# Batch 0's keys and values in eight transfers, the norm factor spread through the two row halves of TensorE, zero matmuls in the first waits, and a new order of all tasks

## The chip, the cores and the metric

The kernel runs on one core of a Trainium2 chip. The metric is the device time of one launch in microseconds. A core has TensorE (matrix products, "PE"; its weight loads are listed apart as "PEld"), VectorE ("DVE"), ScalarE ("ACT") and GpSimd ("POOL"). SyncE ("SP") computes nothing here and issues every DMA transfer.

## The reference

The reference chains two blocks over 8 batches of 576 positions. The first is a linear attention with 8 heads of width 64, followed by a norm over the width:

```
kv  = einsum('bhsd,bhse->bhde', k, v)
out = einsum('bhsd,bhde->bhse', q, kv)
out = out / sqrt(mean(out*out, axis=-1) + 1e-6) * g_norm
```

Its result, laid out as x (576 x 512 per batch), goes into the second block, a mixture of 4 attention experts of which each position uses 2:

```
logits = x @ w_gate                        # the top 2 of 4, softmax of the two
for e in range(4):
    q, k, v = x @ wq[e], x @ wk[e], x @ wv[e]        # 512 -> 64
    a  = softmax(causal(q @ k.T / 8))
    ye = a @ v @ wo[e]                               # 64 -> 512
    out += weight_of_e * ye
```

All inputs and the output are float32.

## The kernel before

Each batch is cut into some 120 named tasks, and the tasks of all batches are written out in three tables: `ORDER` is one sequence of all tasks, `ENGINE` says for each task which engine runs it, and `SLOTS` gives buffers and PSUM banks to the objects in the order in which they are begun. No scheduler moves anything afterwards. Every engine works through its own tasks in the sequence of the table and stands still at a task whose input is not there; SP does the same with its transfers. Most buffers exist twice (`POOLS`), so a transfer into a buffer waits until the last reader of the buffer's former content is done.

The tasks of one batch, with the line under which the profile shows them:

- `lk`, `lv` (line 373) and `lq` (380) load k, v and q. K and v lie with 64 row groups doubled over 128 partitions, so a load has two pieces of 1024 and 1280 bytes per row. Batches 1 to 7 load all 8 heads with each piece. Batch 0 has two parts (`k_parts`), and each part takes heads 0 and 1 (or 2 and 3) and heads 4 and 5 (or 6 and 7) in pieces of 2 heads: 16 transfers.
- `kv` (393) is the product k'v per head. Heads 0 to 3 go to the lower 64 columns of TensorE, heads 4 to 7 to the upper 64; consecutive matmuls alternate between the two. The profile counts two matmuls for each one in the program here. `kvc` and four `ks` (314 on ScalarE, 318 on VectorE) copy the result out of PSUM.
- `qt` (413) transposes half of q on VectorE, `out` (425) multiplies it with kv, `oc` (314, 318) copies the result to `oT`, and `sq` (447, 449) squares it.
- `gl` and `ms` (456) sum gate products and squares over the width. `ln`, `rs`, `na`, `nb`, `nc`, `yh`, `r2` (467 to 494) turn the sums into 1/rms, one Newton step included. The result `r` is 128 x 160: 8 heads x 4 strips on the partitions' rows, positions in strips of 32.
- `sp` (550), the spread, brings 1/rms onto the 128 rows of two heads: for each pair of heads four matmuls against a selection matrix `ssel`, one for each strip, of 128 rows and 160 columns. `xm` (563) multiplies it with `oT` on VectorE and gives `xT`.
- `qp`, `kp` (593) and `v` (575) are the projections, `sc` (616) the scores, with two experts in the two 64-row halves of TensorE, `exp` (628) and `msk` (636) the masked exponential, `pv` (649) its product with v, `rc`, `iv`, `os` (663 to 673) the scaling, `ot` (691) a transpose, `y` (707) the last product, `yc` its copy and `st` (715, 718) the store.

Before the first `kv` stand 12 matmuls on a tile of zeros (734), as `ZEROS` says. The weights are loaded by `lw` (346) and scaled by the norm's weights by `ws` (352, 354), six of them; `lwg`, `lg` and `wgs` do this for the gate.

Of the kernel before, what the change touches and what calls it, by code (L numbers as in the profile page):

```python
# [43 lines left out]
ENGINE = (
    "SSVSASVSVSVSASASVSPSSSSSSTTAVVAAVVTTAAVVAPVPTTAAVVVVVVVVVPAVVVVVTVTVTVTVTATATATATVTAPTAPTAPTAPTVVVTV"
    "VVTVTATATAPTAPTAPTAPTVPVTVVVTATASTASTVSTVSSSSSTAVAAAVVTTVPVPVAAATTAAAVVVVVVVVPAVVVVVTVTVTVTVTATVTATA"
    "TATAPTAPTAPTAPTVPVTVPVTATATVTAPTAPTAPTAPTVVVTVVVTVTASTASTVSTASTASSSSSTAVAVVVVTTVPAPAAAATTAAVVVAVVVVV"
    "PAVVVVVTVTVTVTVTATVTVTATVTAPTAPTAPTAPTVVVTVPVTATVTATAPTAPTAPTAPTVVVTVPVTATASTASTVSTASSSSSTVVVAVVVTTV"
    "AAPVAVATTAAVVVVVVVVVPAVVVVPTVTVTVTVTVTATVTVTVTAPTAPTAPTAPTVVVTVPVTVTATVTAPTAPTAPTAPTVPVTVVVTATASTAST"
    "ASTASTASSSSSTAAAVAVVTTAAAVVAAVTTAAAVVAVVVVVVAVPVVPTVTVTVTVTATVTATATVTAPTAPTAPTAPTVPVTVPVTATATATAPTAP"  # L50
    "TAPTAPTVPVTVVVTVTASTVSTASTASSSSSTAVVAVVVTTAVVPAPVATTAAVVVVVVVVVPAVVVVVTVTVTVTVTVTVTVTATATAPTAPTAPTAP"
    "TVPVTVVVTATATATAPTAPTAPTAPTVVVTVVVTATASTVSTASTVSTVSSSSSTAVAAVVVTTAAAAAPVVTTAAVVVAVVVVVVAVPVVVTVTVTVT"
    "VTVTVTATATATAPTAPTAPTAPTVPVTVVVTVTVTATAPTAPTAPTAPTVPVTVPVTATASTVSTASTASSSSSTVVVAAVVTTVVAPVVAATTAAVVV"
    "AVVVVVPAVPVVPTVTVTVTVTVTATATATATAPTAPTAPTAPTVVVTVVVTVTVTATATAPTAPTAPTAPTVPVTVVVTATATASTASTVSTASTAS"
)
# [10 lines left out]
def k_parts(b):  # L66
    return [(0,), (1,)] if b == 0 else [(0, 1)]
# [6 lines left out]
def names(nb):  # L74
# [5 lines left out]
    for b in range(nb):  # L80
# [6 lines left out]
        out += [(m, b) for m in ("r2", "glr", "glt", "lgs")]  # L87
# [12 lines left out]
def objects(n):  # L100
# [27 lines left out]
        "r2": lambda: [("sm", b), ("r2", b)],  # L128
# [35 lines left out]
def kernel(  # L164
# [614 lines left out]
```

## Time and profile before

| | us |
|---|---|
| median of 3 runs (223.63 to 227.99) | 224.07 |
| the profiled execution | 224.8 |
| its span, first to last instruction | 222.6 |
| TensorE busy / weight loads | 197.2 / 163.0 |
| VectorE, ScalarE, GpSimd busy | 144.4, 124.9, 54.1 |

The mean granted clock of TensorE is 0.951 of full speed. DMA moves 40.32 MB, 181 GB/s over the span. A busy time sums an engine's own work; matmuls overlap in their pipeline, so the share of a busy TensorE is not that of its peak. The chain of waits follows the end of the program back, at each step to what released it.

### The profile page before, as it was taken

Reading aid. Unit: us, or ns where it says so; the run is one execution under the profiler, and the core shown is the slowest. Engines: PE = TensorE matmul, PEld = TensorE weight load, DVE = VectorE, ACT = ScalarE, POOL = GpSimd, SP = SyncE. Lnnn points to the kernel's source line nnn. Section 1 sums busy time; section 2 is a strip of 40 time slices with the busy share of each in tenths; the row PEclk is TensorE's granted clock in tenths of the full one; section 3 lists DMA queues with packets and bytes.
Section 4 is the critical chain, followed back from the end, with each engine's and each line's share of the span. In section 5 each row is a group of like instructions: output and inputs, shape, how many; then the busy total and the mean of one; then the engine's idle time right before and its main releaser. Section 6 shows DMA issues by size and latency. Waiting matters only on the chain.

```text
span 222.6 us, 7257 instructions
## 1 busy us (share of the span) xinstructions
PE 197.2 (89%) x3030; PEld 163.0 (73%) x3044; DVE 144.4 (65%) x368; ACT 124.9 (56%) x222; POOL 54.1 (24%) x146
## 2 busy tenths in 40 slices
PE   7447749998999999999996999998999999999990
PEld 2235449686888878996895878987798869997850
DVE  5103974939769697947766887785685966663370
ACT  2001311676666773378634575377945887768951
POOL 3800400322512440004100253022410341333400
PEclk9855976999999999999999999999999999999998
DMA  6889989999942949597837714001014016004175
GB/s 189 234 222 271 377 178 325 356 334 377 334 170 76 343 141 314 190 299 232 291 62 257 257 50 140 19 3 52 1 70 168 3 40 198 3 0 144 68 271 183
DMA packets 31984, 40.32 MB, mean 181 GB/s; under 512 B 8656, under 2 KB 25040, under 8 KB 31952
## 3 DMA queue, kind: packets, MB, share of 16 engines
q1 hardware_dynamic: 31952, 39.86, 55.8%
q8 instruction: 24, 0.39, 0.8%
q14 instruction: 8, 0.07, 0.1%
HBM read 30.42 MB, written 9.44 MB: 179 GB/s over the span
## 4 chain that ended last, share of the span: by engine, by line
PE 65%; DMA 8%; DVE 7%; ACT 5%; issue 2%; SPq 1%; ACTq 0%; DVEq 0%
PE banks L593 14%; PE banks L616 7%; PE banks L550 7%; DMA v_b<-in_v_dram 7%; PE banks L575 7%; PE banks L456 6%; PE banks L649 6%; PE banks L425 6%; PE banks L393 6%; PE banks L707 5%; ACT PT L628 3%; DMA out_dram<-y 2%; PE banks L691 1%; DVE wgs L338 1%; DVE sq L449 1%
## 5 line engine op out<-in xcount | busy, mean ns | idle before, releaser
L628 ACT ACTIVATE PT<-banks 128x1024 bf16<-128x1024 f32 (+1 forms) x64 | 50.7, 837 | 10.8 <-PE banks L616 9.8
L636 POOL TENSOR_SCALAR_AFFINE_SELECT PT<-PT 128x256 bf16<-128x256 bf16 (+1 forms) x80 | 29.4, 391 | 56.6 <-ACT PT L628 52.9
L563 DVE TENSOR_TENSOR xT<-oT,banks 128x640 fp32r<-128x640 f32 x32 | 25.6, 815 | 12.3 <-PE banks L550 11.6
L393 PE MATMUL banks<-v_b,k_b 128*64 128x64 f32 x640 | 24.5, 241 | 6.3 <-DMA k_b<-in_k_dram 3.2
L393 PEld LDWEIGHTS banks<-v_b,k_b 128*64 128x64 f32 x640 | 22.9, 155 | 9.0 <-issue 7.3
L550 PE MATMUL banks<-r,ssel 128*128 128x160 f32 x128 | 21.3, 302 | 3.0 <-DVE r L494 3.0
L575 PE MATMUL banks<-wv_r,xT 128*128 128x256 f32 x160 | 22.9, 286 | 0.1
L413 DVE STREAM_TRANSPOSE qT<-q_b 128x1152 f32<-128x1152 f32 x16 | 21.8, 1365 | 1.6 <-DMA q_b<-in_q_dram 1.6
L425 PE MATMUL banks<-qT,kvx 32*64 32x288 f32 x256 | 20.5, 439 | 2.7 <-ACT kvx L314 1.6
L550 PEld LDWEIGHTS banks<-r,ssel 128*128 128x128 f32 x128 | 18.3, 208 | 6.1 <-DVE r L494 3.3
L616 PE MATMUL banks<-qs,kT 64*128 64x64 f32 (+4 forms) x192 | 21.4, 339 | 0.7 <-DVE kT L318 0.7
L593 PE MATMUL banks<-xT,wk_r 128*128 128x288 f32 x128 | 21.2, 306 | 1.0 <-DVE oT L318 0.5
L449 POOL TENSOR_TENSOR sq<-oT 128x576 f32<-128x576 f32 x11 | 12.6, 1152 | 34.5 <-DVE oT L318 18.7
L575 PEld LDWEIGHTS banks<-wv_r,xT 128*128 128x128 f32 x160 | 20.1, 189 | 0.9 <-ACT PT L628 0.7
L593 PE MATMUL banks<-xT,wq_r 128*128 128x288 f32 x128 | 20.5, 301 | 0.0
L593 PEld LDWEIGHTS banks<-xT,wk_r 128*128 128x128 f32 x128 | 17.8, 188 | 3.0 <-DVE oT L318 1.0
L425 PE MATMUL banks<-qT,kvs 32*64 32x288 f32 x256 | 19.8, 440 | 0.0
L616 PEld LDWEIGHTS banks<-qs,kT 64*128 64x128 f32 x192 | 14.3, 185 | 7.0 <-issue 0.9
L707 PE MATMUL banks<-wo_b,OT 128*128 128x512 bf16 x58 | 16.8, 380 | 2.8 <-ACT OT L314 1.9
L318 DVE COPY kvs<-banks 32x128 f32<-32x128 f32 x17 | 4.8, 285 | 21.9 <-ACT kvs L314 19.2
L314 ACT COPY kvs<-banks 32x128 f32<-32x128 f32 x15 | 3.9, 257 | 26.4 <-PE banks L393 19.6
L649 PE MATMUL banks<-vx,PT 128*128 128x65 bf16 x480 | 18.3, 193 | 0.2 <-DVE osc L673 0.2
(93 smaller groups left out, 310.2 us busy)
## 6 DMA issues: line engine op xcount, KB each, us to landing
q_b<-in_q_dram SPq DMA_DIRECT2D x16, 576.0 KB, 5.9
out_dram<-y SPq DMA_DIRECT2D x32, 256.0 KB, 2.4
v_b<-in_v_dram SPq DMA_DIRECT2D x7, 640.0 KB, 8.0
k_b<-in_k_dram SPq DMA_DIRECT2D x7, 640.0 KB, 7.8
v_b<-in_v_dram SPq DMA_DIRECT2D x7, 512.0 KB, 6.8
k_b<-in_k_dram SPq DMA_DIRECT2D x7, 512.0 KB, 6.8
out_dram<-y SPq DMA_DIRECT2D x8, 128.0 KB, 2.4
k_b<-in_k_dram SPq DMA_DIRECT2D x4, 160.0 KB, 4.1
```

The source lines that it names most:

```text
L393: nc.tensor.matmul(p_kv[c * Dh : (c + 1) * Dh, (2 * odd + r) * Dh : (2 * odd + r + 1) * Dh], lhsT=kv_in["k"][slot("k", b)][:, h, col], rhs ...
L413: nc.vector.transpose(qTs[slot("qT", b, h)][:].rearrange("p j d -> p (j d)"), q_in[slot("q", b, h)][:].rearrange("p j d -> p (j d)"),)
L425: nc.tensor.matmul(two("out", b, h, a // 2)[r * Dh : (r + 1) * Dh, a % 2, 0:n].rearrange("p (j g) -> p j g", g=NG), lhsT=kvx[rows, 2 * (a ...
L550: nc.tensor.matmul(p_s[:, s, 0:SW], lhsT=ssel[:, s, 2 * c : 2 * c + 2, :].rearrange("p h d -> p (h d)"), rhs=r2s[slot("r2", b)][:], start= ...
L563: nc.vector.tensor_tensor(out=by_strip(xTs[slot("xT", b)][:, c, :]), in0=by_strip(oTs[slot("oT", b)][:, c, :]), in1=p_s.rearrange("p s (i ...
L575: nc.tensor.matmul(bank("v", b, u)[:, n * E * Hd : (n + 1) * E * Hd], lhsT=x[:, c, i * P : (i + 1) * P], rhs=w_r["v"][:, c, :, :].rearrang ...
L593: nc.tensor.matmul(p_p[:, s, 0:HALF], lhsT=w_r[nm][:, c, 2 * pr : 2 * pr + 2, :].rearrange("p e f -> p (e f)"), rhs=x[:, c, s * HALF : (s ...
L616: nc.tensor.matmul(p_s[:, el, o : o + hi - lo], lhsT=kTs[slot("kT", b, pr)][pp, kb * P : (kb + 1) * P], rhs=qss[slot("qs", b, pr)][pp, lo:hi],
L628: nc.scalar.activation(PTs[slot("PT", b, pr)][:, :, d0 : d0 + o], two("sc", b, pr, j)[:, :, 0:o], ACTF.Exp, scale=scale)
L636: nc.gpsimd.affine_select(out=d, in_=d, compare_op=AluOpType.is_ge, fill=0.0, base=0, pattern=[[0, 2], [1, w]], channel_multiplier=-1,)
L649: nc.tensor.matmul(p_O[:, (2 * n + el) * (Hd + 1) : (2 * n + el + 1) * (Hd + 1)], lhsT=PT[:, el, col : col + P], rhs=vx[:, kb, 2 * pr + el ...
L707: nc.tensor.matmul(p_y, lhsT=lhs, rhs=wo_b[:, pr, :], start=(pr == 0), stop=(pr == EP - 1))
```

## The change

- Batch 0's two parts are now heads 0 to 3 and heads 4 to 7, each loaded by one transfer per piece: eight transfers for k and v. A `kv` part of batch 0 is therefore the work of one column half; in the other batches the alternation is as before.
- The spread: a new task `rx` on VectorE multiplies `r` (now an intermediate) by a 0/1 mask of even and odd strips and writes it as 128 x 320. One spread is now two matmuls of 64 rows and 320 columns, one in each row half, for four of 128 rows and 160 columns. `ssel` shrinks to a quarter, and `xm` reads the same amount in another order.
- `ZEROS` now has 17 zero matmuls before the first `kv` part and 1, 5, 1, 1, 3 and 2 before later tasks of batches 0 and 1 (13 together).
- `ORDER`, `ENGINE` and `SLOTS` are new throughout.

```diff
-ZEROS = {('kv', 0, 0): 12}
+ZEROS = {('kv', 0, 0): (17, 0), ('kv', 0, 1): (1, 1), ('out', 0, 1): (5, 1), ('out', 0, 0): (1, 1), ('gl', 0): (1, 4), ('kv', 1, 0): (3, 5), ('out', 1, 0): (2, 2)}
 ORDER = (
-    "0O0J0L0P0X0M0K0Q0U0V0T0S0R0Z0e0N0W0g0Y0f0a0b0100020c0d0i0h0j0k0l052G2O060m0n0o0p0q0r0s16171410121513"
+    "0K0J0L0P0M0Q0U0S0R0V0T0O0N0X0Z0e0g0W0Y0a0001020f0c0d0b0h0i0j0k0l0m0n0o0p2F0s2G2J2K2H2P2I2L2O2M2N2R2V"
...
-    ssel = const.tile([P, 4, H, Dh], FP32R, name="ssel")
-    for s in range(4):
-        nc.gpsimd.tensor_copy(out=ssel[:, s], in_=u8[:, s, :].unsqueeze(2).to_broadcast([P, H, Dh]))
+    ssel = const.tile([P, H, Dh], FP32R, name="ssel")
+    nc.gpsimd.tensor_copy(out=ssel[:], in_=u8[:].unsqueeze(2).to_broadcast([P, H, Dh]))
+
+    odd = const.tile([P, 2], FP32, name="odd")
+    nc.vector.tensor_reduce(
+        odd[:], ident_f[:].rearrange("p (u s x) -> p s u x", u=2, s=2), axis=AX_XY, op=AluOpType.add
+    )
...
-            for c in range(2):
-                if len(k_parts(b)) == 1 and c:
-                    continue
-                h0, h1 = (0, H) if len(k_parts(b)) == 1 else (4 * c + 2 * i, 4 * c + 2 * i + 2)
-                queue(("l" + m, b, i)).dma_start(
...
+            h0, h1 = k_parts(b)[i][0] * H // 2, (k_parts(b)[i][-1] + 1) * H // 2
+            dst = t[:, x, h0:h1, 0 : hi - lo]
...
+            queue(("l" + m, b, i)).dma_start(dst, s_)
...
-        for odd in k_parts(b)[i]:
-            for r in range(2):
-                for j in range(K5):
-                    for c in range(2):
-                        h, col = 4 * c + 2 * odd + r, slice(j * Dh, (j + 1) * Dh)
...
+        for m in range(4):
+            for j in range(K5):
+                for c in k_parts(b)[i]:
+                    h, col = 4 * c + m, slice(j * Dh, (j + 1) * Dh)
...
+    def rx(b):
+        ew(("rx", b)).tensor_tensor(
+            out=r2s[slot("r2", b)][:],
+            in0=sm(b, "r")[:].bitcast(FP32).rearrange("p (i t) -> p i t", t=32).unsqueeze(2).to_broadcast([P, NB, 2, 32]),
+            in1=odd[:].unsqueeze(1).unsqueeze(3).to_broadcast([P, NB, 2, 32]), op=AluOpType.mult,
         )
...
     def spread(b, c):
-        p_s = two("sp", b, c).rearrange("p b (s x) -> p (b s) x", s=2)
-        for s in range(4):
+        for u in range(2):
+            rows = slice(u * Dh, (u + 1) * Dh)
             nc.tensor.matmul(
-                p_s[:, s, 0:SW], lhsT=ssel[:, s, 2 * c : 2 * c + 2, :].rearrange("p h d -> p (h d)"),
-                rhs=r2s[slot("r2", b)][:], start=True, stop=True, skip_group_check=True,
+                two("sp", b, c)[:, u, 0 : 2 * SW], lhsT=ssel[rows, 2 * c : 2 * c + 2, :].rearrange("p h d -> p (h d)"),
+                rhs=r2s[slot("r2", b)][rows].rearrange("p i s t -> p (i s t)"), start=True, stop=True,
+                skip_group_check=True,
             )
```

Three places of the new order follow, as the program lists them; numbers behind a name tell buffers apart.

SP, from its first transfer on, before (the batch of a load is told by its buffers: k_b_90 and v_b_92 hold batch 0, k_b_91 and v_b_93 batch 1):

```order
L380 DMA q_b_98<-in_q_dram 128x1152
L373 DMA k_b_90<-in_k_dram 64x2x256 x2
L373 DMA k_b_90<-in_k_dram 64x2x320 x2
L373 DMA v_b_92<-in_v_dram 64x2x256 x2
L373 DMA v_b_92<-in_v_dram 64x2x320 x2
...
L380 DMA q_b_100<-in_q_dram 128x1152
L332 DMA g_88<-in_g_norm_dram 64x1 x2
L328 DMA wg_in<-in_moe_w_gate_dram 128x4x4
...
L373 DMA v_b_93<-in_v_dram 64x8x256
L373 DMA v_b_93<-in_v_dram 64x8x320
L373 DMA k_b_91<-in_k_dram 64x8x256
```

and now (k_b_89 and v_b_91 hold batch 0, k_b_90 batch 1, and batch 1's v goes into v_b_91 again):

```order
L380 DMA k_b_89<-in_k_dram 64x4x256
L380 DMA k_b_89<-in_k_dram 64x4x320
...
L380 DMA v_b_91<-in_v_dram 64x4x256
L380 DMA v_b_91<-in_v_dram 64x4x320
...
L384 DMA q_b_97<-in_q_dram 128x1152
L384 DMA q_b_98<-in_q_dram 128x1152
L336 DMA wg_in<-in_moe_w_gate_dram 128x4x4
L340 DMA g_87<-in_g_norm_dram 64x1 x2
L380 DMA k_b_90<-in_k_dram 64x8x256
L380 DMA k_b_90<-in_k_dram 64x8x320
L380 DMA v_b_91<-in_v_dram 64x8x256
L380 DMA v_b_91<-in_v_dram 64x8x320
```

The first q, which went out ahead of everything, now follows k and v, with the other half of q behind it; k, v and q of batch 1 go ahead of all the weights but the gate's; and batch 1's v no longer has a buffer of its own, but that of batch 0's v.

VectorE in the norm chain of batch 0, from the copy `yh` (CAST sm_yh) on, before:

```order
L318 CAST sm_yh_126<-sm_y_123 128x160
L494 SCALAR_TENSOR_TENSOR r_0_118<-sm_yh_126,negm,sm_y_123 128x160
L500 TENSOR_TENSOR sm_glr_124<-banks,sm_y_123 128x160
L505 STREAM_TRANSPOSE sm_glt_125<-sm_glr_124 128x160
L563 TENSOR_TENSOR xT_114<-oT_110,banks 128x4x5x32 x4
L508 TENSOR_REDUCE sm_lg_127<-sm_glt_125 128x5x4
```

and now:

```order
L326 CAST sm_yh_125<-sm_y_122 128x160
L511 TENSOR_TENSOR sm_glr_123<-banks,sm_y_122 128x160
L416 STREAM_TRANSPOSE qT_102<-q_b_99 128x1152
L326 COPY kvs_106<-banks 32x128
L416 STREAM_TRANSPOSE qT_101<-q_b_100 128x1152
L362 TENSOR_SCALAR wv_r<-y_177,g_87 128x4x128
L497 SCALAR_TENSOR_TENSOR sm_r_126<-sm_yh_125,negm,sm_y_122 128x160
L504 TENSOR_TENSOR r_0_117<-sm_r_126,odd 128x320
L326 COPY oT_109<-banks 128x2x16x18
```

R2 followed the copy at once; now two q transposes and a k-v copy of batch 1 and the scaling of wv stand between, and rx (128x320) behind it.

TensorE from the norm sums of batch 0 (sq, hsel) to the first projections, before:

```order
L456 MATMUL banks<-sq_112,hsel 32x160 x16
L550 MATMUL banks<-r_0_118,ssel 128x160 x16
L393 MATMUL banks<-v_b_93,k_b_91 64x64 x40
L593 MATMUL banks<-xT_114,wq_r 128x288 x8
...
L425 MATMUL banks<-qT_102,kvx_105 64x288 x2
L593 MATMUL banks<-xT_114,wk_r 128x288 x8
L593 MATMUL banks<-xT_114,wq_r 128x288 x8
L456 MATMUL banks<-oT_110,wgs 32x160 x16
```

and now:

```order
L459 MATMUL banks<-sq_111,hsel 32x160 x16
...
L745 MATMUL banks<-zeros 128x512
L396 MATMUL banks<-v_b_91,k_b_90 64x64 x40
...
L428 MATMUL banks<-qT_101,kvx_104 64x288 x2
L562 MATMUL banks<-r_0_117,ssel 128x320 x4
L459 MATMUL banks<-oT_109,wgs 32x160 x16
L562 MATMUL banks<-r_0_117,ssel 128x320 x4
L459 MATMUL banks<-sq_111,hsel 32x160 x16
L605 MATMUL banks<-xT_113,wq_r 128x288 x8
L587 MATMUL banks<-wv_r,xT_113 128x256 x4
```

Batch 1's k-v and output products moved from behind the spread to ahead of it, and batch 1's sums from behind three projections to ahead of the first one.

## Rows read from the trace of the kernel before

**Rows 1.** Chain of waits, shares of the span summed by line.

```profile
by line: PE banks L593 14.3%; PE banks L616 7.0%; PE banks L550 6.6%; DMA v_b<-in_v_dram 6.5%; PE banks L575 6.5%; PE banks L456 6.4%; PE banks L649 6.3%; PE banks L425 5.7%; PE banks L393 5.6%; PE banks L707 5.2%; ACT PT L628 2.7%; issue 1
```

**Rows 2.** Busy time by stage: length; PE, PEld, DVE, ACT, POOL; PEclk, DMA share, GB/s.

```profile
0.00:38.00 38.00, 24.19 (x316) 17.42 (x316) 17.46 (x36) 4.87 (x9) 8.74 (x29) 0.73 0.87 254
30.00:35.00 5.00, 4.13 (x26) 3.98 (x28) 3.32 (x8) 0.00 (x0) 0.00 (x0) 0.51 0.69 150
35.00:40.00 5.00, 5.00 (x96) 4.50 (x102) 2.38 (x5) 1.42 (x5) 0.00 (x0) 0.81 1.07 367
38.00:214.00 176.00, 170.46 (x2706) 144.58 (x2716) 125.05 (x327) 117.70 (x208) 45.37 (x117) 1.00 0.50 164
```

**Rows 3.** Timeline of TensorE, 0 to 20 us: start, length, work, idle before and releaser.

```profile
1.26 5.17 PE L734 MATMUL banks<-zeros 128*128 128x512 bf16 x12 [1.26 <-DVE zeros L216]
...
9.78 2.39 PE L393 MATMUL banks<-v_b,k_b 128*64 128x64 f32 x38 [0.65 <-DMA v_b<-in_v_dram]
...
15.85 2.40 PE L393 MATMUL banks<-v_b,k_b 128*64 128x64 f32 x38 [0.22 <-DMA k_b<-in_k_dram]
19.90 0.74 PE L425 MATMUL banks<-qT,kvx 32*64 32x288 f32 x2 [1.65 <-ACT kvx L314]
```

**Rows 4.** Busy time of three single microseconds, columns as in rows 2.

```profile
10.00:11.00 1.00, 1.00 (x22) 1.00 (x22) 0.00 (x0) 0.00 (x0) 0.89 (x6) 0.50 0.80 234
23.00:24.00 1.00, 0.71 (x24) 0.11 (x8) 0.91 (x3) 0.23 (x1) 1.00 (x2) 0.88 1.08 367
30.00:31.00 1.00, 0.13 (x1) 0.13 (x1) 0.93 (x4) 0.00 (x0) 0.00 (x0) 0.53 0.44 87
```

**Rows 5.** Chain of waits of the start: start, length, work.

```profile
25.31 2.58 PE banks L456 x64
27.92 0.40 ACT sm_ln L467
...
30.43 0.40 DVE r L494
30.87 2.01 PE banks L550 x8
```

**Rows 6.** Timeline of TensorE: first projection of batch 0.

```profile
38.05 1.32 PE L593 MATMUL banks<-xT,wq_r 128*128 128x288 f32 x8
```

**Rows 7.** Timeline of SP's issues: four k pieces of 2 heads, two of 8.

```profile
1.25 2.71 SPq L373 DMA_DIRECT2D k_b<-in_k_dram  x4
...
31.63 1.31 SPq L373 DMA_DIRECT2D k_b<-in_k_dram  x2
```

**Rows 8.** Chain of waits later on, TensorE's pieces.

```profile
62.75 2.48 PE banks L393 x80
...
84.77 2.31 PE banks L456 x64
...
102.31 0.44 PE banks L616 x2
102.75 2.32 PE banks L425 x64
...
193.06 1.22 PE banks L616 x14
```

**Rows 9.** Groups by line: busy us, mean ns of one, idle before.

```profile
L563 DVE TENSOR_TENSOR xT<-oT,banks 128x640 fp32r<-128x640 f32 x32 | 25.6, 815 | 12.3 <-PE banks L550 11.6 <-ACT PT L628 0.6
...
L413 DVE STREAM_TRANSPOSE qT<-q_b 128x1152 f32<-128x1152 f32 x16 | 21.8, 1365 | 1.6 <-DMA q_b<-in_q_dram 1.6
...
L449 DVE TENSOR_TENSOR sq<-oT 128x576 f32<-128x576 f32 x7 | 6.2, 879 | 0.1
...
L318 DVE COPY kvs<-banks 32x128 f32<-32x128 f32 x17 | 4.8, 285 | 21.9 <-ACT kvs L314 19.2 <-PE banks L393 2.0 <-ACT kvx L314 0.3
...
L487 DVE TENSOR_TENSOR sm_y<-sm_h,sm_y 128x160 f32<-128x160 f32 x8 | 2.6, 319 | 0.2
...
L354 DVE TENSOR_SCALAR wk_r<-y,g 128x512 fp32r<-128x512 f32 x2 | 0.9, 464 | 0.0
```

More of the change, by code (lines that the diff above doesn't have):

```diff
@@ L43 @@
+    "FXFhFiFfFgFj"
 )
 ENGINE = (
[L45 to L49, printed above, removed]
@@ L63 @@
+    "1113510102160022300006130400160204763012474024067220146100321060041713401612510121604100405263020001"
+    "0150620143562024000610303610401614531100111601020161004020607100210462014105362104067014401274601125"
+    "1006001360240023161711210471042624060200073452001311000761441100604003720630442611046027005002101400"
+    "5602104270124610041230110602111600121462005762041602461240430000610463200111236301410642301116703240"
+    "21150043161372124506033241"
 )
@@ L86, in names @@
         out += [(m, b) for m in ("gl", "ms", "ln", "rs", "na", "nb", "nc", "yh")]
-        out += [(m, b) for m in ("r2", "glr", "glt", "lgs")]
+        out += [(m, b) for m in ("r2", "rx", "glr", "glt", "lgs")]
         out += [(m, b) for m in ("m8", "sh", "ex", "mk", "gt", "den", "rd", "gate")]
@@ L127, in objects @@
         "yh": lambda: [("sm", b)],
-        "r2": lambda: [("sm", b), ("r2", b)],
+        "r2": lambda: [("sm", b)],
+        "rx": lambda: [("sm", b), ("r2", b)],
         "glr": lambda: [("b1", "ms", b), ("sm", b)],
@@ L233 @@
         nc.gpsimd.memset(by_head(hsel, r), 1.0)
-    u8 = const.tile([P, 4, H], FP32, name="u8")
+    u8 = const.tile([P, H], FP32, name="u8")
     nc.vector.tensor_reduce(
-        u8[:], ident_f[:].rearrange("p (s h e) -> p s h e", s=4, h=H)[:, :, :, 0:2], axis=AX_X, op=AluOpType.add
+        u8[:], ident_f[:].rearrange("p (s h e) -> p h s e", s=4, h=H)[:, :, :, 0:2], axis=AX_XY, op=AluOpType.add
     )
-    ssel = const.tile([P, 4, H, Dh], FP32R, name="ssel")
-    for s in range(4):
-        nc.gpsimd.tensor_copy(out=ssel[:, s], in_=u8[:, s, :].unsqueeze(2).to_broadcast([P, H, Dh]))
+    ssel = const.tile([P, H, Dh], FP32R, name="ssel")
[4 more added lines that the diff above has]
+    )
     negm = const.tile([P, 1], FP32, name="negm")
@@ L276 @@
     for j in range(n_of["r2"]):
-        r2s.append(const.tile([P, SP // 4], FP32R, name=f"r2_{j}"))
+        r2s.append(const.tile([P, NB, 2, 32], FP32R, name=f"r2_{j}"))
     SW = SP // 4
@@ L282 @@
         small[-1]["yh"] = const.tile([P, SW], FP32R, name=f"sm_yh{j}")
+        small[-1]["r"] = const.tile([P, SW], FP32R, name=f"sm_r{j}")
         t = const.tile([P, NB, 8], FP32, name=f"sm_lg{j}")
@@ L494, in r2 @@
         nc.vector.scalar_tensor_tensor(
-            out=r2s[slot("r2", b)][:], in0=sm(b, "yh")[:].bitcast(FP32), scalar=negm[:, 0:1], in1=sm(b, "y")[:],
+            out=sm(b, "r")[:], in0=sm(b, "yh")[:].bitcast(FP32), scalar=negm[:, 0:1], in1=sm(b, "y")[:],
             op0=AluOpType.mult, op1=AluOpType.add,
+        )
+    def rx(b):
[3 more added lines that the diff above has]
+            in1=odd[:].unsqueeze(1).unsqueeze(3).to_broadcast([P, NB, 2, 32]), op=AluOpType.mult,
         )
@@ L556, in halves, with by_half @@
         return t[:, 0:S].rearrange("p (s n) -> p s n", s=2)
-    def by_strip(t):
-        return t.rearrange("p (i s t) -> p s i t", s=4, t=32)
+    def by_half(t):
+        return t.rearrange("p (i u t) -> p u i t", u=2, t=Dh)
     def xm(b, c):
-        p_s = two("sp", b, c).rearrange("p b (s x) -> p (b s) x", s=2)[:, :, 0:SW]
         nc.vector.tensor_tensor(
-            out=by_strip(xTs[slot("xT", b)][:, c, :]), in0=by_strip(oTs[slot("oT", b)][:, c, :]),
-            in1=p_s.rearrange("p s (i t) -> p s i t", t=32), op=AluOpType.mult,
+            out=by_half(xTs[slot("xT", b)][:, c, :]), in0=by_half(oTs[slot("oT", b)][:, c, :]),
+            in1=two("sp", b, c)[:, :, 0 : 2 * SW].rearrange("p u (i t) -> p u i t", t=Dh), op=AluOpType.mult,
         )
@@ L729, with zero_matmuls @@
     )
-    def zero_matmuls(n, count):
-        key = next(key for key in objects(n) if key[0] in ("b1", "b2"))
+    def zero_matmuls(count, n):
         for _ in range(count):
             nc.tensor.matmul(
-                banks[:, slot_of[key], :], lhsT=zeros[:, 0:P], rhs=zeros[:], start=True, stop=True,
-                skip_group_check=True,
+                banks[:, n, :], lhsT=zeros[:, 0:P], rhs=zeros[:], start=True, stop=True, skip_group_check=True
             )
```

79 lines of the change are left out of this document (39 added, 40 removed).

## The prediction

> **What bounds the kernel now.** I read the chain of waits summed by line first, then busy time by stage, then the start piece by piece. The profiled execution took 224.8 us, 222.6 of it span; the median of the runs is 224.07, so 0.7 comes off at the end. The chain is TensorE's own work with a DMA share from the first third [rows 1]. The stages say where each rules [rows 2]: from 38 to 214 us TensorE is busy 170.46 of 176 us, so 5.5 us of idle is all that a better order can find there, and work taken off TensorE counts nearly in full. VectorE has 125.05 and ScalarE 117.70 us of work in the same stretch. From 0 to 38 TensorE is busy 24.19 us, and DMA moves 254 GB/s where it reaches 367 later. The start is waiting.
>
> The start in detail: the two halves of batch 0's k-v product begin at 9.78 and 15.85, both released by DMA, and the output product at 19.90 [rows 3]. The granted clock was full when the zero matmuls ended, 0.50 from 10 us until the 23rd, then full, and 0.50 again from the 30th, after TensorE had stood through the norm chain [rows 4, 5]. The first projection of batch 0 starts at 38.05 [rows 6]. That is my marker: before it waits count, after it TensorE's work.
>
> **Part 1, the start.** *Transfers.* Before, the first q transfer goes out ahead of sixteen k and v ones. One k or v issue holds SP 0.68 us at 2 heads (2.71 for four) and 0.66 at 8 heads (1.31 for two) [rows 7]: the cost is per transfer, not per byte. Eight end at 0.8 + 8 x 0.67 = 6.2 us. The bytes are 2.36 MB (2 x 576 x 512 x 4), at 350 GB/s (a little under the stage from 35 to 40 us [rows 2]) 6.7 us; I let them run from 1.5 us on and add 1 us to complete: all landed by 9.2. By the rate of the first stage (254) it is 11.8.
>
> *The k-v product.* A part is now one column half alone, where before the two halves alternated. At the full clock 80 matmuls took 2.48 us [rows 8], 0.031 each, so 40 cost between 1.24 us (were the alternation worth nothing) and 2.48 (were pairs wholly side by side). No row shows one half alone; I take 2.48: the output product, float32 too, does 64 matmuls of 288 columns in 2.32 us [rows 8], eight side by side as it is coded (4 row strips, 2 column halves), 0.29 a round or 1.0 ns a column, by which 64 columns are 0.064, twice 0.031. At half clock it is up to 5.0. The 17 zero matmuls cost nothing: 12 took 5.17 us [rows 3], 17 end by 8.6 at the latest, about when the first four k and two v transfers have landed. So part one runs from about 8 to 10.5, part two to 13.0, if the clock holds, against 18.25 before.
>
> *To the norm.* Then 1.65 us until the output product [rows 3], at 14.7; the q halves, now after k and v, have their 1.18 MB by 12.6 + 1, and two transposes of 1.37 us [rows 9] end about 15.5, just covering it. The output product takes 2.32 at full clock [rows 8] where it took 3.8 at half: done at 17.1, before 23.7. The gap to the norm sums was 1.6, and they take 2.58 [rows 5]: 21.3. From there the chain to r2's start took 2.5 us (27.92 to 30.43) [rows 5]: 23.8.
>
> *The new queue on VectorE.* Here r2 no longer follows at once. Ahead of it stand two q transposes of batch 1, a k-v copy and a weight scaling, and rx comes behind it: 1.37 + 0.28 + 1.37 + 0.46 + 0.40 + 0.53 = 4.4 us [rows 5, 9]. Rx (128x320) I price between a 128x160 product, 0.319, and a 128x576 one, 0.879 [rows 9], near the middle by size. So the spread starts at 28.2, if the data are there: k, v and q of two batches and the first wv are 7.3 MB, at 350 GB/s 21 us, landed by about 24. Queued behind the waiting r2 on VectorE is an oT copy of batch 1, and TensorE waits for rx; but TensorE fills the wait with batch 1's k-v and output products. Four xm of 0.815 [rows 9] with that copy and a spread take 4.4: the first projection starts at 32.6 instead of 38.05, and by then the output product and norm sums of batch 1 (2.32 + 2.31, [rows 8]) are done, which before came later. Gain 5.4 + 4.6 = 10.0. The other end: k-v parts at half clock and the following stage partly so, some 6 to 7 us back, gain 3. I take 8.5, since the 13 later zero matmuls stand in just the waits in which the clock fell before, but each stands only at the head of its wait.
>
> **Part 2, the spread.** On the chain line 550 has 6.6% of 222.6 = 14.7 us [rows 1]; less 2.0 of batch 0 [rows 5] it is 12.7 for 26 tasks (its pieces there hold 104 matmuls), 0.49 each; all 28 tasks of batches 1 to 7 take 13.7. The new form (two matmuls of 64 rows, 320 columns, one in each row half) is that of the score matmuls. Two of 512 columns by themselves kept TensorE 0.44 us, fourteen with 1664 columns per half 1.22 [rows 8]. One after the other, fourteen would need 2 x 1664 / 2.4 GHz = 1.39, so the halves do run side by side. The difference, six pairs and 1152 columns (0.48 us) in 0.78, leaves 0.05 a pair. A spread within a run of such tasks costs 0.13 + 0.05 = 0.18; alone 0.44 - 0.08 = 0.36. In the order most spreads stand next to score tasks: there were 23 runs of score tasks, and there are 29 runs of score tasks and spreads. So 28 x 0.18 + 6 x 0.18 = 6.1, saved 7.6; at the lone price everywhere 10.1, saved 3.6. I take 7.
>
> **Part 3, what is added.** Seven more rx, 0.53 each, 3.7 us on VectorE, covered by its 51 us of idle in the stage [rows 2]; uncovered 3.7. POOL loses three weight-spreading copies at setup, where nobody waits; zero. With 7 us less on TensorE the other two engines, at 71 and 67% of the stage, show through more often, and every task has a new place. Between an idle that vanishes in part (-1) and one that doubles (+5) I take +2.
>
> **Sum.** 224.8 - 8.5 - 7 + 2 = 211.3, against the median 210.6; I say **211 us**. All good ends: -10 -7.6 -1, 205.5. All bad ones: -3 -3.6 +5, 222.5.
>
> **Rivals.**
> *A, the drain.* Each spread pays for leaving and entering the 64-row form: 0.36 for all 28, gain 3.6. For it: the lone pair takes twice its streaming time. Against it: 26 spreads of 32 join a run. Time 224.1 - 8.5 - 3.6 + 2 = 214. The Trainium skill states it as a rule in "TensorEngine Tiling (Array Packing)", section Tiling Modes, Key Properties: changing the tiling mode, not just the tile, drains TensorE. By that rule the count of changes decides, and the trace's 0.44 for a lone pair agrees with it.
> *B, the cold start.* The clock falls in spite of the zero matmuls, the unpaired parts cost 5.0 each, part two ends at 18 as before, and half of part 1 is gone. For it: the fall in [rows 4] came after gaps that are still there in part. Gain 3 to 4 instead of 8.5: 216.
> *C, slower.* Batch 1's v goes into the buffer of batch 0's v. SP therefore stands at that transfer until part two of the k-v product is done, and q of batch 1 and all weights are queued behind it, 3.9 MB with that v. R2 waits on VectorE behind the transposes of that q, and the first projection needs wq. If part two ends at 18 as before and those bytes come at 150 GB/s, as in the stage from 30 to 35 us [rows 2], the last of the weights lands at 45 and the first projection starts at 46. That is 8 later than before with 4.6 of work ahead; with the spread's 7 gained and 5 of idle lost the time is 224.8 + 8 - 4.6 - 7 + 5, about 226. With idle at +2 it decides from a first projection at 47.6 on, with +5 from 44.6. For it: SP's order, and that slow stage held weights too. Against it: k of batch 1 goes ahead of the stall and fills it, and the stages around the slow one moved more, 367 GB/s in the next one.
> *D, nothing from the order.* The idle doubles and the start is cold, with the spread anywhere between its ends: 224.1 - 3.5 + 5 - 7 or - 3.6, 219 to 222.
>
> **How the numbers follow.** Forecast (206 to 213) 0.57; A 0.14, B 0.16, D 0.08, C 0.05. What a measurement can tell is 2%, 219.6 to 228.6. Forecast, A and B lie under it, D half: faster 0.87 by the cases; I leave 0.86, same 0.10, slower 0.04. The range takes the forecast with its good end, A, B: 205 to 218.
>
> **What would show it.** Right: the second half of k-v starts before 11 us and ends near 13; the granted clock stays full from about 8 us on; the spread of batch 0 starts near 28 and the first projection near 33; in the sums by line the spread falls from 14.7 to some 7 us; VectorE's rx rows near 0.53 us with nobody on TensorE waiting for them after batch 0; TensorE's idle from there to its last 10 us at 5 to 8 us. Wrong: granted clock 0.50 in the k-v rows (B); spread pieces of 0.36 throughout (A); SP standing at batch 1's v past 14 us, and TensorE released by wv or q of batch 1 (C); new waits of TensorE for VectorE or ScalarE that add up to over 5 us (D).

## The result and the profile after

Before 224.88 us (223.63 to 227.99, four runs), after **213.12 us** (211.51 to 215.01, four runs): a ratio of 0.947 (95% interval 0.937 to 0.957). The forecast was 211, range 205 to 218. The profiled execution of the changed kernel is the slowest of its four (215.01 us, span 213.3, mean granted clock 0.971; the other three have spans of 209.8 to 211.7 and clocks of 0.982 to 0.994). A second profile of the same kernel stands in experiment 5.

First the stages, with the columns of [rows 2]:

```profile
0.00:38.00 38.00, 32.66 (x461) 21.18 (x462) 17.20 (x37) 12.47 (x27) 8.21 (x27) 0.91 0.82 238
38.00:205.00 167.00, 161.17 (x2518) 132.22 (x2518) 120.79 (x321) 111.27 (x195) 49.67 (x124) 0.99 0.51 175
```

TensorE is busy 32.66 of the first 38 us where it was 24.19, and its idle in the long stage is 5.83 us where it was 5.54. The stage is 9 us shorter, the start is fuller; 10.3 us of its work are zero matmuls, which were 5.2 before. Now TensorE's start (columns of [rows 3]; the output products are left out):

```profile
1.26 6.25 PE L745 MATMUL banks<-zeros 128*128 128x512 bf16 x17 [1.26 <-DVE zeros L219]
10.44 4.50 PE L396 MATMUL banks<-v_b,k_b 128*64 128x64 f32 x40 [2.93 <-DMA v_b<-in_v_dram]
...
15.40 2.98 PE L396 MATMUL banks<-v_b,k_b 128*64 128x64 f32 x40
...
24.60 1.29 PE L459 MATMUL banks<-sq,hsel 128*32 128x160 f32 x32
...
33.44 0.56 PE L562 MATMUL banks<-r,ssel 64*128 64x320 f32 x4
...
37.07 1.32 PE L605 MATMUL banks<-xT,wq_r 128*128 128x288 f32 x8
```

The zeros end at 7.51, and TensorE stands 2.93 us until the data land. Part one takes 4.50 us at 0.50 of the clock, and part two ends at 18.38 instead of 13.0. The norm sums are done at 25.9 instead of 21.3. The marker, the first projection, stands at 37.07; it was 38.05 [rows 6].

The granted clock in these stretches (next to last three columns: PEclk, DMA share, GB/s):

```profile
7.00:9.00 2.00, 0.51 (x3) 0.01 (x1) 0.00 (x0) 0.00 (x0) 0.00 (x0) 1.00 0.99 301
9.00:11.00 2.00, 0.56 (x6) 0.60 (x7) 0.00 (x0) 0.00 (x0) 0.00 (x0) 0.64 1.02 361
11.00:13.00 2.00, 2.00 (x21) 2.00 (x21) 0.00 (x0) 0.00 (x0) 0.00 (x0) 0.50 1.02 419
17.00:19.00 2.00, 2.00 (x28) 1.58 (x27) 0.02 (x1) 0.55 (x3) 0.00 (x0) 1.00 0.14 46
50.00:54.00 4.00, 3.69 (x65) 3.01 (x61) 1.79 (x3) 1.20 (x4) 0.00 (x0) 0.57 1.08 357
```

The granted clock reads full while the zeros run (their pace says more: they start 0.43 us apart up to 5.9 us and 0.22 apart from 6.3 on), falls in the gap behind them, is back by 17, and falls once more at 50 after a wait for batch 2's v (below). The row from 17 to 19 shows rival C's stall too: DMA moves 46 GB/s, because SP stands at batch 1's v until the first buffer is free:

```profile
18.30 1.30 SPq L380 DMA_DIRECT2D v_b<-in_v_dram  x2
```

The spread's matmuls of the long stage (line 562; PE, PEld, PEclk, DMA share, GB/s), and two of its pieces in the chain of waits:

```profile
38.00:205.00 167.00, 10.55 (x56) 5.61 (x56) 0.99 0.51 175
```

```profile
169.47 0.35 PE banks L562 x2
170.57 0.14 PE banks L562 x2
```

The same stage of the kernel before, line 550:

```profile
38.00:214.00 176.00, 17.55 (x112) 14.78 (x112) 1.00 0.50 164
```

28 spreads cost 10.55 us of busy time for 17.55. Busy time includes the overlap with neighbouring matmuls in the pipeline, so I also summed the time from each spread matmul's start to that of the next matmul (or to its own end, where a wait follows): 14.3 us before, 8.1 after, 0.51 and 0.29 for a spread. Of the two pieces the first heads a run of score matmuls (0.35) and the second ends it (0.14); neither stands alone.

What TensorE waits for between 38 and 205 us (sum, times, longest), and VectorE's added work:

```profile
PE banks L396 <- DMA v_b<-in_v_dram: 2.0, 1, 2.0
```

```profile
L504 DVE TENSOR_TENSOR r<-sm_r,odd 128x320 fp32r<-128x320 f32 x8 | 4.0, 502 | 0.1
```

No wait for rx (line 504) is among TensorE's waits: eight of 0.50 us are hidden, as forecast at 0.53.

### The profile page after: what moved, and what is told of

Read it like the earlier page. It is cut to its first block, busy times and chain, and to the rows that moved or that the text cites. A ratio compares the mean times of both kernels' runs of the same rounds, so it can differ in the third digit from the quotient of the medians.

```text
span 213.3 us, 7162 instructions
## 1 busy us (share of the span) xinstructions
PE 197.0 (92%) x2998; PEld 154.6 (72%) x2998; DVE 140.5 (66%) x363; ACT 126.1 (59%) x226; POOL 58.3 (27%) x153
## 5 line engine op out<-in xcount | busy, mean ns | idle before, releaser
L396 PE MATMUL banks<-v_b,k_b 128*64 128x64 f32 x640 | 26.6, 236 | 5.5 <-DMA v_b<-in_v_dram 4.9
L396 PEld LDWEIGHTS banks<-v_b,k_b 128*64 128x64 f32 x640 | 25.2, 149 | 8.3 <-issue 7.8
L452 POOL TENSOR_TENSOR sq<-oT 128x576 f32<-128x576 f32 x15 | 17.1, 1152 | 33.9 <-ACT oT L322 27.3
L628 PE MATMUL banks<-qs,kT 64*128 64x64 f32 (+4 forms) x192 | 22.9, 340 | 0.2
L322 ACT COPY kvs<-banks 32x128 f32<-32x128 f32 x21 | 5.4, 257 | 26.6 <-PE banks L396 24.7
L719 PE MATMUL banks<-wo_b,OT 128*128 128x512 bf16 x72 | 19.9, 381 | 0.5 <-ACT kvs L322 0.5
L428 PE MATMUL banks<-qT,kvs 32*64 32x288 f32 x256 | 18.5, 410 | 0.0
L661 PEld LDWEIGHTS <-PT 128*128 128x128 bf16 x480 | 15.7, 97 | 3.6 <-issue 2.5
L605 PEld LDWEIGHTS banks<-xT,wq_r 128*128 128x128 f32 x128 | 17.5, 188 | 0.9 <-ACT sm_y L473 0.4
L322 ACT COPY oT<-banks 128x576 f32<-128x576 f32 x20 | 12.6, 644 | 8.7 <-PE banks L428 8.7
```

The lines of the kernel that those rows point to most:

```text
L322: nc.scalar.copy(dst, src)
L396: nc.tensor.matmul(p_kv[c * Dh : (c + 1) * Dh, m * Dh : (m + 1) * Dh], lhsT=kv_in["k"][slot("k", b)][:, h, col], rhs=kv_in["v"][slot("v", ...
L428: nc.tensor.matmul(two("out", b, h, a // 2)[r * Dh : (r + 1) * Dh, a % 2, 0:n].rearrange("p (j g) -> p j g", g=NG), lhsT=kvx[rows, 2 * (a ...
L605: nc.tensor.matmul(p_p[:, s, 0:HALF], lhsT=w_r[nm][:, c, 2 * pr : 2 * pr + 2, :].rearrange("p e f -> p (e f)"), rhs=x[:, c, s * HALF : (s ...
L628: nc.tensor.matmul(p_s[:, el, o : o + hi - lo], lhsT=kTs[slot("kT", b, pr)][pp, kb * P : (kb + 1) * P], rhs=qss[slot("qs", b, pr)][pp, lo:hi],
L661: nc.tensor.matmul(p_O[:, (2 * n + el) * (Hd + 1) : (2 * n + el + 1) * (Hd + 1)], lhsT=PT[:, el, col : col + P], rhs=vx[:, kb, 2 * pr + el ...
```

## The experiments

The ratios are against the kernel before, timed on the same chip.

**1. The new order with the old spread.** `rx` leaves VectorE; four matmuls of 128 rows stand where two of 64 did.

```
-        for u in range(2):
-            rows = slice(u * Dh, (u + 1) * Dh)
+        for s in range(4):
...
-                rhs=r2s[slot("r2", b)][rows].rearrange("p i s t -> p (i s t)"), start=True, stop=True,
+                rhs=r2s[slot("r2", b)][:], start=True, stop=True, skip_group_check=True,
```

> The changed kernel with the spread put back to four matmuls of 128 rows and 160 columns (no mask product; rx writes 1/rms directly), order and all else as changed. Work theory: TensorE bounds the middle, so the 6 us by which the spread's pieces shrank come back nearly in full: 218.5 to 220 (about 0.975 of before). Rival, slack: after the start the other engines and transfers set the pace and TensorE's saving is absorbed: 213 to 215 (0.95 to 0.955).

Measured: 219.29 us, ratio 0.980 (0.974 to 0.986). Beside the change's 0.947 that is 0.033 of 224 us, 7.4 us (by the two intervals, about 5 to 10), for the spread alone. Line 553 in the long stage (PE, PEld, PEclk, DMA share, GB/s), and TensorE's zeros and marker:

```profile
36.00:211.00 175.00, 18.13 (x112) 14.49 (x112) 1.00 0.50 172
```

```profile
1.26 6.58 PE L736 MATMUL banks<-zeros 128*128 128x512 bf16 x17 [1.26 <-DVE zeros L219]
...
36.43 1.33 PE L596 MATMUL banks<-xT,wq_r 128*128 128x288 f32 x8
```

The old spread's 18 us are back, and the marker stands near where it stood in the changed kernel's first profile (36.43 against 37.07). From start to start the old spread costs 15.8 us here, 0.56 each, and 14.3 in the old order: the new form saves 7.7 us in the new order and, as the next experiment shows, 4.8 in the old one.

**2. The new spread in the old order.** The kernel before with `rx` behind `r2` and two matmuls of 64 rows.

```
-        for s in range(4):
+        for u in range(2):
+            rows = slice(u * Dh, (u + 1) * Dh)
...
+                rhs=r2s[slot("r2", b)][rows].rearrange("p i s t -> p (i s t)"), start=True, stop=True,
```

> The kernel before with only the new spread (mask product right behind r2 on VectorE, two matmuls of 64 rows per spread), order as before. Work theory: a gain of 4 to 6 us, less than in the new order since here a spread seldom stands beside a score task, so most pay the lone price of 0.35 us instead of about 0.5: 219 to 221 (0.975 to 0.985). Drain rival: entering and leaving the 64-row form eats it, 222 to 225.

Measured: 222.61 us, ratio 0.993 (0.989 to 0.998): some 1.5 us. Line 560, then two stretches of the whole core (columns of [rows 2]):

```profile
36.00:214.00 178.00, 10.91 (x56) 5.16 (x56) 0.99 0.49 164
```

```profile
36.00:214.00 178.00, 170.94 (x2662) 138.15 (x2673) 129.01 (x335) 117.50 (x208) 45.49 (x117) 0.99 0.49 164
...
119.00:123.00 4.00, 4.00 (x19) 3.45 (x18) 2.40 (x6) 0.64 (x1) 0.23 (x1) 0.57 0.80 228
```

The busy time of the spread falls as in the change (10.91), and its time from start to start by 4.8 us (14.3 to 9.5; most spreads stand between tasks of 128 rows here and cost 0.34 or 0.35). From the marker on nothing comes of it: 185.0 us (36.70 to the end at 221.7) where the kernel before has 184.55. In the same sums, idle grew by 1.5 us and the projections by about 2, most of it the fall of the clock from 119 to 123, which leaves over 1 us that I cannot place. This is one profile, among the slower of the ten runs (223.46 us); that the old order, written for the old durations, keeps the gain from being collected is my reading of it and not shown by a run of its own.

**3. Without the later zeros.** Only the 17 zeros ahead of the first k-v part remain.

```
-ZEROS = {('kv', 0, 0): (17, 0), ('kv', 0, 1): (1, 1), ('out', 0, 1): (5, 1), ('out', 0, 0): (1, 1), ('gl', 0): (1, 4), ('kv', 1, 0): (3, 5), ('out', 1, 0): (2, 2)}
+ZEROS = {('kv', 0, 0): (17, 0)}
```

> The changed kernel with the 17 zero matmuls before the first k-v part and without the 13 later ones. Clock theory: without them the granted clock falls again somewhere between 17 and 33 us, as it did before at 30, and the stage to the first projection takes 2 to 4 us longer: 215 to 217. Rival: the waits there are bridged by batch 1's work anyway, and the zero matmuls only stood in the way: 212.5 to 213.5, no change.

Measured: 210.7 us, ratio 0.938 (0.930 to 0.947). The interval overlaps the change's (0.937 to 0.957), so a gain is not shown, but a loss of 2 to 4 us is excluded. In the profiled run, the fastest of four, the granted clock held to TensorE's last matmul without the 13 zeros, so they are not needed to hold it; the other three have mean clocks of 0.980 to 0.990, and no trace says where they fell. The profiled run shows the start at full clock, TensorE and then VectorE:

```profile
1.25 5.75 PE L745 MATMUL banks<-zeros 128*128 128x512 bf16 x17 [1.25 <-DVE zeros L219]
10.38 4.67 PE L396 MATMUL banks<-v_b,k_b 128*64 128x64 f32 x80 [3.38 <-DMA v_b<-in_v_dram]
...
29.20 0.57 PE L562 MATMUL banks<-r,ssel 64*128 64x320 f32 x4
```

```profile
24.76 1.37 DVE L416 STREAM_TRANSPOSE qT<-q_b 128x1152 f32<-128x1152 f32 x1
26.16 0.29 DVE L326 COPY kvs<-banks 32x128 f32<-32x128 f32 x1
26.48 1.38 DVE L416 STREAM_TRANSPOSE qT<-q_b 128x1152 f32<-128x1152 f32 x1
27.79 0.45 DVE L362 TENSOR_SCALAR wv_r<-y,g 128x512 fp32r<-128x512 f32 x1
28.15 0.38 DVE L497 SCALAR_TENSOR_TENSOR sm_r<-sm_yh,negm,sm_y 128x160 fp32r<-128x160 f32 x1
28.56 0.49 DVE L504 TENSOR_TENSOR r<-sm_r,odd 128x320 fp32r<-128x320 f32 x1
```

The forecast's queue on VectorE is here, task for task: from the first transpose at 24.76 to the end of rx at 29.05 it takes 4.3 us (forecast 4.4). The marker is at 32.83 (forecast 32.6). The zeros ended earlier here (7.0) than in the profile after (7.5), and the clock held all the same.

**4. Sixteen transfers in the new order.** Each k or v piece of batch 0 is cut in two again.

```
+            if b == 0:
+                for g in (0, 2):
+                    queue(("l" + m, b, i)).dma_start(dst[:, g : g + 2], s_[:, g : g + 2])
```

> The changed kernel with batch 0's k and v again in sixteen transfers of 2 heads (each part still one column half). Issue theory: SP needs 10.5 us instead of 5.5 for them, the first k-v part starts 3 to 4 us later, q likewise, and the delay runs through to the end: 216 to 217. Rival: the bytes set the time of landing, not the issues, and the first part starts within 1 us of where it did: 213 to 214.

Measured: 214.25 us, ratio 0.956 (0.949 to 0.963), which is not told apart from the change (0.947, 0.937 to 0.957). SP's issues, then TensorE:

```profile
0.81 5.36 SPq L382 DMA_DIRECT2D k_b<-in_k_dram  x8
6.21 5.22 SPq L382 DMA_DIRECT2D v_b<-in_v_dram  x8
```

```profile
1.26 6.75 PE L749 MATMUL banks<-zeros 128*128 128x512 bf16 x17 [1.26 <-DVE zeros L219]
10.56 4.06 PE L400 MATMUL banks<-v_b,k_b 128*64 128x64 f32 x40 [2.55 <-issue]
```

SP issues until 11.43 instead of 6.36, and part one starts at 10.56 instead of 10.44. That does not show that the bytes alone set the start. A v transfer took, from issue to landing (KB each, median us), here and then in the changed kernel:

```profile
v_b<-in_v_dram SPq DMA_DIRECT2D x4, 128.0 KB, 3.0
```

```profile
v_b<-in_v_dram SPq DMA_DIRECT2D x2, 256.0 KB, 5.8
```

With sixteen, part one's last v transfer goes out at about 8.8 and lands soon; DMA moves 214 GB/s from 3 to 9 us and 1.76 MB by 10.44, which is what stands in the queue up to that transfer. With eight it goes out by about 5.1 and lands late, among later transfers: 286 GB/s and 2.27 MB. The two starts agree, but the first is held up by the issues and the second by the shared rate. Eight transfers with q held back until part one has landed were not run.

**5. The changed kernel again**, unaltered, beside the next ones.

> The changed kernel once more, unaltered, on the chip of the next three. Clock theory: the time scatters by 3 to 4 us with the moment at which the granted clock steps; where a profile shows the clock falling between 9 and 12 us the first projection starts near 37, where it holds near 33. Median 211.5 to 213.5 (0.943 to 0.957). Rival, transfers: the start is set by when batch 1's data land and is the same whatever the clock did, within 1 us.

Measured: 212.35 us, ratio 0.947 (0.940 to 0.955), span 209.9. In this run the clock held over the first gap:

```profile
10.36 2.52 PE L396 MATMUL banks<-v_b,k_b 128*64 128x64 f32 x40 [3.07 <-DMA v_b<-in_v_dram]
13.12 2.54 PE L396 MATMUL banks<-v_b,k_b 128*64 128x64 f32 x40 [0.25 <-issue]
...
30.71 0.56 PE L562 MATMUL banks<-r,ssel 64*128 64x320 f32 x4
...
34.34 1.33 PE L605 MATMUL banks<-xT,wq_r 128*128 128x288 f32 x8
```

The same instructions, 2.7 us earlier at the marker than in the profile after. Beside experiment 3, whose first part starts at the same time and whose clock held too, the spread is 1.5 us later (30.71 against 29.20): the zeros behind the first part are the only edit between the two, one profile of each. The marker moved with the clock, so the forecast's rival (the same start whatever the clock did) falls.

**6. A bridge of zeros.** 32 zeros ahead of the first k-v part, until the data are there, and none later.

```
-ZEROS = {('kv', 0, 0): (17, 0), ('kv', 0, 1): (1, 1), ('out', 0, 1): (5, 1), ('out', 0, 0): (1, 1), ('gl', 0): (1, 4), ('kv', 1, 0): (3, 5), ('out', 1, 0): (2, 2)}
+ZEROS = {('kv', 0, 0): (32, 0)}
```

> The changed kernel with 32 zero matmuls before the first k-v part instead of 17 and none later, so that TensorE works without a gap until the data land at 10.4 us. Clock theory: the granted clock no longer falls at 10 us, both parts of the k-v product take 2.4 us each, the first projection starts at 33 in every profile, median 209 to 210.5. Rival: the clock falls at another of the waits (15 to 17 or 23 to 29 us), 212 to 214.

Measured: **209.49 us** (209.19 to 209.77), ratio 0.932 (0.927 to 0.937), the narrowest scatter of all:

```profile
1.26 9.30 PE L745 MATMUL banks<-zeros 128*128 128x512 bf16 x32 [1.26 <-DVE zeros L219]
10.49 4.70 PE L396 MATMUL banks<-v_b,k_b 128*64 128x64 f32 x80
...
32.96 1.33 PE L605 MATMUL banks<-xT,wq_r 128*128 128x288 f32 x8
```

The granted clock stays full to TensorE's last matmul, and the mean clock is 0.996 to 1.000 in all four runs. This version beats both kernels; beside experiment 5, on the same chip, the intervals do not touch. Of the 2.4 us between the two profiled spans 1.4 lie before the marker. The rest lies behind it, where the second fall of the clock (at 50 us in the profile after, from 46 in experiment 5) is absent. How much the 32 zeros give without the removal of the 13 is not shown: against experiment 3 (0.938) the intervals overlap.

**7. The bridge, and batch 1's v in its own buffer**, so that SP need not wait for part two.

```
+                    if key[0] == "v":
+                        slot_of[key] = begun_v[0] % 2
+                        begun_v[0] += 1
```

> As e6_bridge, and the v loads alternate between the two buffers, so that batch 1's v no longer waits for the k-v product of batch 0. Stall theory: SP issues it at 11.7 instead of 15, all that stands behind it comes 3 us earlier, TensorE's wait of 2 us for batch 2's v goes, the first projection comes 0 to 1 us earlier since VectorE's queue (4.4 us behind the norm) then sets it: 1.5 to 3 us faster than e6_bridge, 207 to 209. Rival: the transfers were already limited by rate, and the stall only shifted who waits: same as e6_bridge within 1 us.

Measured: 209.62 us, ratio 0.932 (0.926 to 0.939), no gain. SP's issues here, then in experiment 6:

```profile
11.41 2.77 SPq L381 DMA_DIRECT2D v_b<-in_v_dram  x2
...
16.15 6.70 SPq L355 DMA_DIRECT2D y<-in_moe_wv_dram  x4
```

```profile
15.10 1.30 SPq L380 DMA_DIRECT2D v_b<-in_v_dram  x2
...
18.55 3.83 SPq L354 DMA_DIRECT2D y<-in_moe_wv_dram  x4
```

Batch 1's v goes out 3.7 us earlier, but its two issues now hold SP 2.77 us and those of wv 6.70, so wv is out at 22.85 against 22.38. In experiment 6 DMA moves 356 GB/s from 11.4 to 15.1, while SP stands: the transfers already move at their rate, and an earlier request only waits elsewhere. (The zeros also end 0.4 us later here, at 10.95, and the marker is at 33.48 against 32.96.)

**8. The same, and batch 0's k-v product as one**, alternating between the column halves once all its data are there.

```
+        if len(k_parts(b)) == 2 and i == 0:
+            return
...
-                for c in k_parts(b)[i]:
+                for c in range(2):
```

> As e7_bridge_own_v, and batch 0's k-v product is done as one task with the column halves alternating, once all eight transfers have landed. Pairing theory: 80 matmuls take 2.5 us instead of 4.7 from about 11.3 instead of 10.4, so it ends 1.3 us earlier, and the first projection moves by as much at most: 0.5 to 1.3 us faster than e7_bridge_own_v. Rival: the last transfer lands so late (12.5 or more) that the head start of part one was worth as much: no change.

Measured: 209.2 us, ratio 0.932 (0.925 to 0.939).

```profile
11.93 2.52 PE L399 MATMUL banks<-v_b,k_b 128*64 128x64 f32 x78 [1.36 <-DMA v_b<-in_v_dram]
...
19.05 1.29 PE L462 MATMUL banks<-oT,wgs 128*32 128x160 f32 x32 [0.87 <-issue]
...
32.97 1.33 PE L608 MATMUL banks<-xT,wq_r 128*128 128x288 f32 x8
```

78 alternating matmuls take 2.52 us where 80 of one half after the other took 4.70, and the norm sums start 0.7 us earlier (19.05 against 19.79). The marker does not move: batch 1's k-v product waits 0.96 us for batch 1's v and starts at 22.48 (22.46 in experiment 6), and VectorE, whose two q transposes stand around a copy of that product, reaches the copy at 26.30 in both.

**9. The bridge in the old kernel.** The kernel before with 29 zeros for 12.

```
-ZEROS = {('kv', 0, 0): 12}
+ZEROS = {('kv', 0, 0): 29}
```

> The kernel before with 29 zero matmuls for 12 ahead of batch 0's k-v product, its order and spread as they were. Theory (the order makes the gain of the start, the clock is an extra): in this order TensorE still waits for the second k-v part, the output product and the norm chain with nothing to do, so bridging the first wait brings at most the first k-v part at full clock (1.2 us) and perhaps the output product (1.5 us): 222 to 224.5, first projection at 36.5 to 38. Rival (the clock makes it): the whole start runs at full clock once the first wait is bridged; both k-v parts take 1.2, the output product 2.3, the spread 2.0, and the first projection starts near 33: 218 to 220.

Measured: 224.15 us, ratio 0.996 (0.991 to 1.000): about 1 us, at most 2.

```profile
9.06 1.81 PE L393 MATMUL banks<-v_b,k_b 128*64 128x64 f32 x40
13.80 2.48 PE L393 MATMUL banks<-v_b,k_b 128*64 128x64 f32 x40 [2.93 <-DMA k_b<-in_k_dram]
...
28.89 3.70 PE L550 MATMUL banks<-r,ssel 128*128 128x160 f32 x16 [3.01 <-DVE r L494]
```

```profile
14.00:21.00 7.00, 5.33 (x96) 3.83 (x102) 2.66 (x5) 1.53 (x4) 0.09 (x1) 0.53 0.93 270
29.00:36.00 7.00, 7.00 (x96) 6.86 (x96) 3.93 (x7) 0.00 (x0) 0.00 (x0) 0.58 0.76 201
```

The first wait is bridged and part one is faster, but TensorE then stands 2.93 us for the second part and 3.01 for r, with no other work in its order, and the clock is at half behind both (0.53 and 0.58). A bridge over one gap is worth little where the order leaves the next two open.

## Why the prediction was right, and where it was not

**The sum.** 211 was forecast, 213.1 measured. In the profiled runs 9.3 us of span went: 1.0 up to the marker and 8.3 behind it.

**Part 1, the start (8.5 forecast, between 3 and 10).** The mechanism held: the marker would come at 32.6, with batch 1's output product and norm sums done before it. Where the clock held and the later zeros were away it came at 32.83 and 32.96 (experiments 3 and 6), a gain of 5.1 to 5.2 us and the 4.6 of work moved ahead. In the changed kernel itself it came at 37.07 and at 34.34 (experiment 5): gains of 5.6 and 8.3 with the same 4.6. The step that failed is the landing of k and v with the zeros ahead of it: "part one runs from about 8 to 10.5". The data landed at 10.1 to 10.6 in every profile with 17 zeros, with eight transfers as with sixteen, so the transfer term was 2.4 us too short. The trace after shows why: 24 GB/s in the first 3 us, where I let the bytes run from 1.5 on; 301 GB/s from 7 to 9 us where I took 350; and, summed over the first 10.44 us, 2.27 MB moved, where only k and half of v, 1.77 MB, stand in the queue up to part one's last transfer. Later transfers share the rate, so the first part does not land ahead of them. And "17 end by 8.6 at the latest, about when the first four k and two v transfers have landed" hid the consequence: the zeros end 2.9 us too soon, and the clock falls in that gap in some runs. This is **rival B** in part: it was one gap, the one ahead of the product. The 13 later zeros, to which the forecast gave credit, are not needed (experiments 3 and 6): without them the kernel took 210.7 us, and with the first gap bridged besides 209.5, two values that their intervals do not tell apart.

**The 2.48 us for a half alone** was right (2.52 and 2.54 at full clock); the reasoning by columns of the output product held.

**Part 2, the spread (7 forecast, between 3.6 and 7.6).** 7.0 by busy time and 6.2 from start to start between the two kernels; within the new order, beside experiment 1, 7.7 from start to start and 7.4 by the runs. The lone price was right: 0.36 forecast, 0.34 or 0.35 in experiment 2. The price beside score tasks, 0.18, was too low. All but one of the 28 spreads stand directly beside a score task, about as the forecast counted, and yet they cost 8.1 us and not 6.1: 19 of them 0.24 to 0.26 each, nine 0.31 to 0.49. That is halfway to the 10.1 of **rival A**. The saving came out near the forecast by luck in part, since the old form, too, costs more in the new order, 15.8 and not 13.7. The Trainium skill, "TensorEngine Tiling (Array Packing)", section Tiling Modes, Key Properties, has a change of tiling mode drain TensorE. The rows agree in direction: 0.35 for a spread that heads a run, 0.14 for one that ends it, 0.34 for a lone one.

**Part 3 (+2, between -1 and +5).** rx is hidden. Idle grew by 0.3 us in the long stage, and the clock's fall from 50 to 54 cost about 1.7 (4 us at 0.57). Of the 8.3 us behind the marker, 4.6 are work moved ahead and 6.2 to 7 the spread, 2.0 came back in this way, which leaves 0.5 to 1.3 us that I cannot place.

**Rival C** is right in its first half: SP stood until part two had ended, at 18.3. But q and the weights still came in time, and taking the stall away changed nothing in the bridged kernel (experiment 7); with the cold start, where DMA fell to 46 GB/s, it was not tried. **Rival D** falls: there is no doubled idle, and the new order with the old spread (experiment 1) is still 2% faster than before.

**What the parts are worth together.** The spread alone gives 1.5 us; the order, with the eight transfers and the zeros, about 4.5 (0.020 of 224); both 11.8. The two need each other: 4.8 and 7.7 us of TensorE's time are what the new spread saves in the old and the new order. The eight transfers are worth no more than can be measured here. What stays open is why the same gap costs the clock in one run and not in the next. The five profiles with 17 zeros only show what goes with it: it held where the zeros took 5.75 and 6.02 us (experiments 3 and 5) and fell where they took 6.25, 6.58 and 6.75 (after, experiments 1 and 4). All five begin with zeros 0.43 us apart; the pace of 0.22 is reached at 5.3 and 5.8 us in the first two and at 6.3, 7.0 and 7.2 in the other three.

## What to carry to other kernels

Where all tasks stand in a hand-written order, price an edit that shortens one engine's tasks together with a new order: here it was worth 1.5 us alone and about 7 in the new one, where the old form itself had become dearer. Fill a wait ahead of the first real work up to the moment the data land, read from the trace and not from the number of transfers; zeros that ended 3 us too soon let the clock fall in three of five profiles, and zeros elsewhere brought nothing that could be measured. Before removing a stall of a queue, ask whether the transfers behind it were already moving at their rate.

## What the runs showed of the hardware

- The granted clock fell behind gaps of 2.3, 2.6 and 2.9 us (experiments 1 and 4, profile after) and held over longer ones of 3.1 and 3.4 us (experiments 5 and 3), in the same place of the program: the length of the gap alone does not decide.
- Float32 matmuls of 64 columns alternating between the two column halves of TensorE ran side by side almost in full: 2.52 us for 78 in pairs, 4.70 for 80 unpaired (experiments 8 and 6).
- A spread of two 64-row matmuls of 320 columns took 0.34 or 0.35 us between tasks of 128 rows (experiment 2) and mostly 0.24 to 0.26 beside score tasks (profile after); four 128-row matmuls of 160 columns took 0.51 on average in the old order and 0.56 in the new (experiment 1).
- The same issue can hold SP twice as long: two v issues took 1.30 us in experiment 6, 3.5 us behind the issue before them, and 2.77 in experiment 7, right behind it; four of wv 3.83 and 6.70. In the kernel before, too, two k issues took 1.31 us at 31.63 and 2.87 at 18.27, so the forecast's price per transfer is not a fixed one.
- At the start, a k transfer's issue held SP 0.67 us with two heads and 0.73 with four (eight in 5.36 us, four in 2.93).
